# A Fourier mixing layer with a low-rank mixer: narrow products set side by side on TensorE, and another channel step for the second batch

## The chip, the cores and the metric

The kernel runs on one core of a Trainium2 chip. The core has five engines with a queue each: TensorE (PE; its weight loads are listed as PEld), VectorE (DVE), ScalarE (ACT), GpSimd (POOL) and SyncE (SP), which here only issues DMAs. The metric is the device time of one execution in microseconds (us).

## The reference

The input `x` is 8 x 3136 x 256 (batch, sequence, channel). The first stage takes the real part of a Fourier transform over sequence and channel; the second is a mixer:

```
X = real(fft(fft(x, axis=1), axis=2))          # per batch 3136 x 256
u = X + V^T (U^T X)                            # low rank, rank 32, over the sequence
out = u + relu(u @ w_ch1) @ w_ch2              # 256 -> 1024 -> 256 channels
```

## The kernel before

**Transform over the sequence.** The real part is cos·cos - sin·sin, and both factors are symmetric, so that 1569 of 3136 output rows and 129 of 256 channels carry everything. For each batch DVE folds `x` along the channels (`along_d`, L344; the middle channel, number 128, is a single column that POOL copies in `alone`, L352), along the sequence (`mirror`, L356), and over two halves (`half`, L360). The result is two tiles `G[b % 2][par]` of eight tiles of 98 or 99 rows each; columns 0 to 127 belong to the sine, 128 to 255 to the cosine, 256 is channel 128 alone. The stationary operand of a product is such a column block of G, the moving one is a row of a cosine or sine table with 393 frequencies and, after them, 32 columns of the transformed U (`tabs`, 425 columns in all, QW). `seq` (L399) does one of eight groups of a batch: par (even or odd frequencies), typ (0 sine, 1 cosine) and pn (odd or even rows). The pn=0 group is copied to `ev` by ACT, the pn=1 group is combined with it on DVE into the tiles `A` (cosine) and `B` (sine).

**Channel 128.** It needs the cosine alone. In batches 0 and 1 (b < B0 = 2) the sine groups get four more products each (L420), with columns 256 to 383 of G as the stationary operand and the cosine table as the moving one; since those columns are zero except the first, the result for channel 128 lands in row 0 of `B`. Batches 2 to 7 take channel 128 together in a *column pass* (`column_steps`, L485): its `x` values come by small DMAs, `fold_c` folds them to `GC[par]` with six columns for each of the eight tiles, and `group` (L507) runs four groups (par, pn) of four products with a stationary operand of six columns. The pn=0 groups are copied by ACT, the pn=1 groups are combined by DVE into `rows`, one row per batch; `finish` mirrors `rows` on ACT and puts the low-rank part into `tabc128`.

**Transform over the channels.** Batch 0 uses `chan` (L535): for four stretches of 392 rows and two halves h, one product of `A` with the cosine matrix `MC` and one of `B` with the sine matrix `MSN` are summed, and the sum is copied to `S` (h=0, by ACT) or `T` (h=1, by DVE). Batches 1 to 7 use `even_ch` (L547) and `odd_ch` (L556): `A` with `ME` is copied to `evd` by ACT, `B` with `MO` stays in PSUM, and DVE forms the sum as S and the difference as T. `across` (L565) then copies rows 64 to 127 of `A`, straight and mirrored, into rows 64 to 127 of `VA[b % 2]`, and for batch 1 also row 0 of `B` (channel 128) into row 32 of it; batches 2 to 7 get row 32 by a DMA from `rows` (L585). For batch 0 `last_row` (L588) writes row 64 of VA on DVE instead. `MO` is `MSN` with its row 0 set to zero by POOL.

**Mixer.** `lowrank` (L573) makes `TA` for a batch. The batches' rows are cut into 49 chunks of 512. `front(c)` (L606) multiplies `VA` with `TA` and DVE adds S or T: that is `u`. `first_product` (L626, eight per chunk, relu on ACT) and `second_product` (L636, four per chunk, on DVE the sum with `u`, which a DMA has transposed) are the mixer.

**Order.** Up to the first chunk the instructions run in the order written (`manual_schedule`, from L99 to `order.close()`, L860); after that a planner orders each engine's queue by its own model of times, starting from the order of the program, and the folds are pinned to the order written. The setup builds the tables (L694 to L813): POOL makes some of them by copies (`mirror_even`, `cosine_odd(4)`), issues the loads (`load_weights`, `load_v`, `load_second`), and runs `alone` for both halves of batch 0. From chunk 0 on each step of the next batch hangs on a slot 8c + j (chunk c, first product j): `spread` (L841) deals the steps of `fold`, `transform` and `column_steps` over a range of slots. Batch 1's transform has slots 23 to 42, the column pass 56 to 68. `front(c + 1)` is issued at j = 3.

**PSUM.** Every product outside the two mixer products takes one of three buffers with the tag "dft": `pt`, `pth`, `ptc`, `pst`, `ptt`, `ph`. A buffer is free again when ACT or DVE has read it for the last time.

In the setup there is already a function that runs narrow products in four groups of 32 output partitions, `transform_u` (L264):

```
for n in range(NI // 2):
    for g in range(4):
        pk, pn = divmod(g, 2)
        i = ktiles(pk)[n]
        nc.tensor.matmul(acc[g * R:(g + 1) * R, :], GU[:kp(i), typ, pn, i, :],
                         tabs[typ][:kp(i), i, pn, :NQ],
                         start=(n == 0), stop=(n == NI // 2 - 1))
```

Of the kernel before, what the change touches and what calls it, by code (L numbers as in the profile page):

```python
# [10 lines left out]
BF16 = mybir.dt.bfloat16  # L11
# [5 lines left out]
P = 128  # L17
PQ = 98
KP = PQ + 1
NI = 8  # L20
# [7 lines left out]
def kernel(  # L28
# [137 lines left out]
    def va_zeros(s):  # L166

        nc.gpsimd.memset(VA[s][R:2 * R].bitcast(I32), 0)
        if s == 0:
            nc.gpsimd.memset(VA[s][2 * R:].bitcast(I32), 0)  # L170

# [12 lines left out]
    ME = cpool.tile([P, P], BF16, name="me")  # L184
    MO = cpool.tile([P, P], BF16, name="mo")
    nc.vector.tensor_scalar(ncol[:], ncol[:], 1.0 / S, 0.0, op0=AL.mult, op1=AL.max)
# [71 lines left out]
    def ktiles(par):  # L258
        return [i for i in range(NI) if (i + 1) % 2 == par]
# [139 lines left out]
    def seq(b, par, typ, pn, parts=(0, 1)):  # L399
# [8 lines left out]
        g = G[b % 2][par]  # L408
        if pn == 0 and (b >= B0 or (b == 1 and typ == 1)):
            halves(d, g, par, typ)  # L410
            return
# [38 lines left out]
    cr = cpool.tile([KP, 2, NI, NB], FP32, name="cr")  # L450
    GC = [cpool.tile([KP, NI, NB], BF16, name=f"gc{par}", tag=f"gc{par}") for par in range(2)]
    rows = cpool.tile([NB, S], BF16, name="rows")
    tabc128 = cpool.tile([P, (NB + 3) * R], BF16, name="tabc128")
    flip = cpool.tile([P, 2, P], BF16, name="flip")
    unit = cpool.tile([P, NB], FP32, name="unit")

    def column_zeros():
        nc.gpsimd.memset(cf[:], 0.0)
        nc.gpsimd.memset(cr[:], 0.0)

    def column_flips():
# [3 lines left out]
    def column_loads():  # L465

        for t, dst, n in ((0, cf, NI - 1), (1, cr, 0)):
# [7 lines left out]
            for b in range(NB):  # L475
                for a in range(2):
# [6 lines left out]
                    yield load  # L483

    def column_steps():  # L485
        ec = cpool.tile([KP, 2, NI, NB], BF16, name="ec")
        tc_ = cpool.tile([NB, 2, R], FP32, name="tc")

        def fold_c():
# [11 lines left out]
            for par in range(2):  # L501
                nc.vector.tensor_tensor(GC[par][:], ec[:, 0], ec[:, 1],
                                        op=AL.add if par == 0 else AL.subtract)
        yield fold_c
        ev = {}

        def group(par, pn):  # L507
            pt = psum.tile([NB, QW], FP32, tag="dft", name="ptc", bufs=3)
            ks = ktiles(pn)
            for n, i in enumerate(ks):  # L510
                nc.tensor.matmul(pt[:], GC[par][:kp(i), i, :], tabs[1][:kp(i), i, par, :],  # L511
                                 start=(n == 0), stop=(n == len(ks) - 1))
            if pn == 0:
                ev[par] = wp.tile([P, QW], FP32, tag="ev", name="evc", bufs=2)
                nc.scalar.copy(ev[par][:NB], pt[:])
                return
            e = ev[par][:NB]
            up = rows[:, HALF // 2 - par:(0 if par else None):-2]
            dn = rows[:, HALF // 2 + 2 - par:HALF + 1 - par:2]
            nc.vector.tensor_tensor(up, pt[:, par:NQ], e[:, par:NQ], op=AL.add)  # L520
            nc.vector.tensor_tensor(dn, e[:, 1:NQ], pt[:, 1:NQ], op=AL.subtract)
            nc.vector.tensor_tensor(tc_[:, par, :], pt[:, NQ:QW], e[:, NQ:QW], op=AL.add)
        for par in range(2):
            for pn in range(2):
                yield lambda par=par, pn=pn: group(par, pn)

        def finish():
            nc.scalar.copy(rows[:, HALF + 1:S], rows[:, HALF - 1:0:-1])
            nc.vector.tensor_tensor(tc_[:, 0], tc_[:, 0], tc_[:, 1], op=AL.add)
            for b in range(NB):  # L530
                nc.vector.tensor_single_scalar(tabc128[:NB, b * R:(b + 1) * R], tc_[:, 0],
                                               unit[:NB, b:b + 1], op=AL.mult)
        yield finish

# [21 lines left out]
    def odd_ch(b, ch):  # L556
        d = ST[b]
        lo = ch * 392 + (1 if ch else 0)
        hi = (ch + 1) * 392 + 1
        pt = psum.tile([P, NQ], FP32, tag="dft", name="pst", bufs=3)  # L560
        nc.tensor.matmul(pt[:, :hi - lo], MO[:], d["B"][:, lo:hi], start=True, stop=True)  # L561
        for k, op in (("S", AL.add), ("T", AL.subtract)):
            nc.vector.tensor_tensor(d[k][:, lo:hi], d["e"][:, :hi - lo], pt[:, :hi - lo], op=op)  # L563

    def across(b, to, src, ch):  # L565

        lo = ch * 392 + (1 if ch else 0)
        hi = (ch + 1) * 392 + 1
        nc.scalar.copy(VA[b % 2][to, lo:hi], src[:, lo:hi])
        lo, hi = max(lo, 1), min(hi, HALF)  # L570
        nc.scalar.copy(VA[b % 2][to, S - hi + 1:S - lo + 1], src[:, hi - 1:lo - 1:-1])

    def lowrank(b):  # L573
        d = ST[b]
        pt = psum.tile([P, 256], FP32, tag="dft", name="ptt", bufs=3)
        n = 0
        for typ in range(2):
            for par in range(2):
                nc.tensor.matmul(pt[:], TAB[:, (2 * typ + par) * R:(2 * typ + par) * R + P],  # L579
                                 MDT[typ][:],  # L580
                                 start=(n == 0), stop=(n == 3 and b < B0))
                n += 1
        if b >= B0:
            nc.tensor.matmul(pt[:], tabc128[:, (b - B0) * R:(b - B0) * R + P], ones[:], start=False, stop=True)
            nc.sync.dma_start(out=VA[b % 2][R:R + 1, :], in_=rows[b - B0:b - B0 + 1, :])  # L585
        nc.scalar.copy(TA[b % 2][:R, :], pt[:R])
# [80 lines left out]
    def transform(b):  # L667

        for par, typ in ([(0, 0), (1, 0), (0, 1), (1, 1)] if b == 0 else
                         [(0, 1), (0, 0), (1, 1), (1, 0)]):  # L670
            for pn in range(2):
                yield lambda par=par, typ=typ, pn=pn: seq(b, par, typ, pn)
        if b == 0:
            for ch in range(4):
                for h in range(2):
                    yield lambda ch=ch, h=h: chan(b, ch, h)
            return
        for ch in range(4):
            yield lambda ch=ch: (even_ch(b, ch), across(b, slice(2 * R, P), ST[b]["A"][2 * R:], ch))
            yield lambda ch=ch: (odd_ch(b, ch),  # L680
                                 b < B0 and across(b, slice(R, R + 1), ST[b]["B"][0:1], ch))
        yield lambda: lowrank(b)
# [29 lines left out]
    cosine_low(1)  # L712
    mirror_even(0, 1)
    load_weights()
    cosine_odd(4)
    halve(0)
# [36 lines left out]

    alone(0, xr, EOR_)
    alone(0, xf, EOF_)
    load_v()
# [8 lines left out]
    ta_rows(0)  # L765
    alone(1, xr, EOR_)
    alone(1, xf, EOF_)
    uc[0]()
# [33 lines left out]
    column_zeros()  # L802
    nc.gpsimd.memset(tabc128[:].bitcast(I32), 0)

    def channel_tables():
# [3 lines left out]
        nc.gpsimd.memset(ME[QD:, 0:1], 0.0)  # L809
        nc.gpsimd.tensor_copy(MO[:], MSN[:, :P])  # L810
        nc.gpsimd.memset(MO[0:1], 0.0)

# [25 lines left out]

    due = {0: steps[6:7], 1: steps[7:8], 2: [lambda: last_row(0), column_flips]}

# [61 lines left out]
```

## Time and profile before

| | |
|---|---|
| median of three runs | 463.79 us (462.05 to 465.17) |
| the profiled execution | 463.73 us |
| its span, from first to last instruction | 462.0 us |
| busy: PE, DVE, ACT, POOL | 444.9, 353.1, 299.8, 69.7 us |
| mean granted clock of TensorE | 0.996 |

A row of the profile gives the start and length in us (or, for groups, the count, the busy time and the mean length in ns of one), the engine, the line of the kernel, the operation, what it writes and reads, and the shape. In brackets stands how long the engine sat idle before, and whose work ended that. A line with `x16` merges 16 instructions that follow one another. A length of a product is longer than its share of PE's time, because products overlap; starts are what to compare. DVE's and ACT's instructions overlap by about 0.1 us too.

### The profile page before, as it was taken

Reading aid. Unit: us, or ns where it says so; the run is one execution under the profiler, and the core shown is the slowest. Engines: PE = TensorE matmul, PEld = TensorE weight load, DVE = VectorE, ACT = ScalarE, POOL = GpSimd, SP = SyncE. Lnnn points to the kernel's source line nnn. Section 1 sums busy time; section 2 is a strip of 40 time slices with the busy share of each in tenths; the row PEclk is TensorE's granted clock in tenths of the full one; section 3 lists DMA queues with packets and bytes.
Section 4 is the critical chain, followed back from the end, with each engine's and each line's share of the span. In section 5 each row is a group of like instructions: output and inputs, shape, how many; then the busy total and the mean of one; then the engine's idle time right before and its main releaser. Section 6 shows DMA issues by size and latency. Waiting matters only on the chain.

```text
span 462.0 us, 8048 instructions
## 1 busy us (share of the span) xinstructions
PE 444.9 (96%) x2988; PEld 290.7 (63%) x2988; DVE 353.1 (76%) x811; ACT 299.8 (65%) x570; POOL 69.7 (15%) x112
## 2 busy tenths in 40 slices
PE   3889999899999999999999999999999999999996
PEld 2544656565666666666666666666666666666665
DVE  8887998886898779977898769977898666433433
ACT  7866537965876568655866577655865586656552
POOL 5992621020022001120022002100000000000000
PEclk9989999999999999999999999999999999999999
DMA  7994898994276824973377736683235323333343
GB/s 217 233 238 111 172 219 200 132 206 96 69 193 197 213 70 132 208 217 92 115 209 201 148 81 161 193 218 111 70 91 115 91 71 115 91 116 92 114 116 113
DMA packets 102955, 67.51 MB, mean 146 GB/s; under 512 B 73526, under 2 KB 99328, under 8 KB 99776
## 3 DMA queue, kind: packets, MB, share of 16 engines
q1 hardware_dynamic: 97906, 41.26, 38.3%
q0 software_dynamic: 4992, 25.74, 19.4%
q8 instruction: 23, 0.38, 0.3%
q14 instruction: 16, 0.13, 0.1%
q10 hardware_dynamic: 18, 0.00, 0.0%
HBM read 29.33 MB, written 25.69 MB: 119 GB/s over the span
## 4 chain that ended last, share of the span: by engine, by line
PE 87%; DVE 5%; POOL 2%; ACT 2%; issue 2%; DVEq 0%; POOLq 0%
PE p L648 35%; PE p L632 34%; PE pt L423 7%; PE ph L612 4%; PE pth L390 2%; DVE eor L348 1%; PE pst L561 1%; DVE eof L348 1%; PE pst L552 1%; DVE u L620 1%; PE ptt L579 1%; PE ptc L511 1%; DVE eos L357 1%; POOL xf L55 1%; ACT tabs L218 0%
## 5 line engine op out<-in xcount | busy, mean ns | idle before, releaser
L634 ACT ACTIVATE h<-p 128x512 bf16<-128x512 f32 x392 | 223.4, 597 | 130.3 <-PE p L632 128.4
L632 PE MATMUL p<-u,w 128*128 128x512 bf16 x784 | 218.8, 379 | 1.0 <-DVE u L620 0.8
L648 PE MATMUL p<-w,h 128*128 128x256 bf16 x1568 | 203.4, 273 | 0.0
L648 PEld LDWEIGHTS <-h 128*128 128x128 bf16 x1568 | 152.9, 98 | 59.9 <-issue 0.5
L632 PEld LDWEIGHTS <-w 128*128 128x128 bf16 x784 | 76.0, 98 | 52.4 <-issue 3.6
L654 DVE TENSOR_TENSOR o<-p,ut 128x4 f32<-128x4 f32 (+1 forms) x100 | 16.3, 163 | 58.8 <-PE p L648 56.3
L55 POOL DMA_INDIRECT xf<-in_x_dram,xidx x16 | 20.9, 1304 | 190.3 <-DVE eof L348 187.1
L657 DVE TENSOR_TENSOR o<-p,ut 128x254 f32<-128x254 f32 (+1 forms) x100 | 40.7, 407 | 0.0
L656 DVE TENSOR_TENSOR o<-p,ut 128x254 f32<-128x254 f32 (+1 forms) x100 | 40.7, 407 | 0.0
L348 DVE TENSOR_TENSOR eor<-xr 99x1024 bf16<-99x1024 f32 x32 | 39.1, 1230 | 0.0
L348 DVE TENSOR_TENSOR eof<-xf 99x1024 bf16<-99x1024 f32 x32 | 38.5, 1217 | 0.0
L620 DVE TENSOR_TENSOR u<-ph,S 128x512 bf16<-128x512 f32 (+15 forms) x64 | 35.1, 557 | 0.0
L620 DVE TENSOR_TENSOR u<-ph,T 128x512 bf16<-128x512 f32 (+15 forms) x64 | 35.0, 557 | 0.0
L423 PEld LDWEIGHTS <-g 98*128 98x128 bf16 (+1 forms) x184 | 18.3, 100 | 19.7 <-issue 2.3
L612 PE MATMUL ph<-va,ta 128*128 128x512 bf16 (+18 forms) x128 | 29.6, 329 | 0.6 <-ACT evd L554 0.6
L563 DVE TENSOR_TENSOR S<-evd,pst 128x392 bf16<-128x392 f32 (+1 forms) x28 | 15.8, 563 | 9.7 <-PE pst L561 7.8
L357 DVE TENSOR_TENSOR eos<-eof,eor 99x1024 bf16<-99x1024 bf16 (+2 forms) x33 | 21.9, 676 | 1.6 <-POOL eof L354 1.5
L423 PE MATMUL pt<-tabc,g 98*128 98x425 bf16 x104 | 22.2, 343 | 0.1
L423 PE MATMUL pt<-tabs,g 98*128 98x425 bf16 x80 | 19.1, 370 | 1.5 <-DVE g L361 1.5
L361 DVE TENSOR_TENSOR g<-eos 99x2048 bf16<-99x2048 bf16 (+3 forms) x20 | 19.8, 1008 | 0.2
L432 DVE TENSOR_TENSOR tab<-pt,ev 128x32 bf16<-128x32 f32 x32 | 6.1, 191 | 17.7 <-PE pt L423 16.7
L563 DVE TENSOR_TENSOR T<-evd,pst 128x392 bf16<-128x392 f32 (+1 forms) x28 | 15.7, 560 | 0.0
(157 smaller groups left out, 332.3 us busy)
## 6 DMA issues: line engine op xcount, KB each, us to landing
out_dram<-o SPq DMA_DIRECT2D x48, 512.0 KB
xr<-in_x_dram POOLq DMA_DIRECT2D x14, 784.0 KB, 6.3
xr<-in_x_dram SPq DMA_DIRECT2D x2, 784.0 KB
ut<-u SPq DMA_TRANSPOSE x49
w<-in_moe_w_ch_dram SPq DMA_DIRECT2D x1, 512.0 KB
w<-in_moe_w_ch_dram POOLq DMA_DIRECT2D x1, 512.0 KB, 5.7
out_dram<-o SPq DMA_DIRECT2D x4, 128.0 KB
va<-in_moe_V_dram POOLq DMA_DIRECT2D x2, 196.0 KB, 5.3
```

What stands on the lines that cost most here:

```text
L55: nc.gpsimd.indirect_dma_start(out_, None, bass.AP(t.tensor, t.offset, [[w, rows], [1, w]]), bass.IndirectOffsetOnAxis(idx, 0), element_of ...
L348: pin(nc.vector.tensor_tensor(dst[:, a, :, part * P:(part + 1) * P].rearrange("p i (k t) -> p i k t", k=2), lo, hi, op=AL.subtract if part ...
L357: pin(nc.vector.tensor_tensor(EOS[:, a, :, cols], EOF_[:, a, :, cols], EOR_[:, a, ::-1][:, :, cols], op=op))
L423: nc.tensor.matmul(pt[:], g[:kp(i), i, col:col + P], tabs[t][:kp(i), i, par, :], start=(n == 0), stop=(n == len(mm) - 1))
L563: nc.vector.tensor_tensor(d[k][:, lo:hi], d["e"][:, :hi - lo], pt[:, :hi - lo], op=op)
L612: nc.tensor.matmul(ph[:, col:col + hi - lo], TA[b % 2][:, s * P:(s + 1) * P], VA[b % 2][:, lo:hi], start=True, stop=True)
L620: nc.vector.tensor_tensor(u[:, s, col:col + hi - lo], ph[:, col:col + hi - lo], src, op=AL.add)
L632: nc.tensor.matmul(p1[:], W1[:, s, j * P:(j + 1) * P], k["u"][:, s, :], start=(s == 0), stop=(s == 1))
L634: LAST[0] = nc.scalar.activation(k["h"][:, j, :], p1[:], AF.Relu)
L648: nc.tensor.matmul(p2[:, t % w, :], h[:, j, rs], W2[:, j, :], start=(j == 0), stop=(j == JT - 1))
L656: nc.vector.tensor_tensor(o[:, ts, 1:P], p2[:, :w, 1:P], ut[:, ts, 1:P], op=AL.add)
L657: nc.vector.tensor_tensor(o[:, ts, P + 1:D], p2[:, :w, P + 1:D], ut[:, tT, P - 1:0:-1], op=AL.add)
```

## The change

- **Narrow products.** A new function `narrow` replaces `group`. It runs all 16 products of a single-channel transform in one step: the four groups (pn, par) write four bands of 32 partitions of one PSUM tile. The stationary operand is 32 columns wide, of which the first nb count. ACT copies the lower 64 partitions (pn = 0) to the upper half of `ev`; two further steps, one for each par, combine the halves on DVE, straight into `dst`. The column pass uses it with six columns; `GC` gets 32 zeroed columns behind it, so that its last block can be read 32 wide.
- **Batch 1's channel 128** leaves the sine groups (four products less in each of four) and uses `narrow` with columns 256 to 287 of G. Its row goes to row 32 of `VA[1]`, mirrored by two ACT copies, and its low-rank part to `low`, so that `lowrank(1)` has a fifth product.
- **Batch 1's channel step** is now `chan`, with both halves copied by ACT, and `last_row(1)`; rows 64 to 127 of `VA[1]` are zeroed by POOL in the setup.
- `MO` goes: `odd_ch` uses `MSN` directly.
- **Order.** In the setup POOL runs `alone` for half 0 before `cosine_odd(4)` and `load_weights`, and for half 1 before `load_v`. `column_flips` (two DVE copies) moves from slot 2 to slot 44. Batch 1's transform has 21 steps instead of 17, the column pass 5 instead of 6, in the same ranges of slots.

```
     def va_zeros(s):
         nc.gpsimd.memset(VA[s][R:2 * R].bitcast(I32), 0)
-        if s == 0:
-            nc.gpsimd.memset(VA[s][2 * R:].bitcast(I32), 0)
+        nc.gpsimd.memset(VA[s][2 * R:].bitcast(I32), 0)
...
-            if b < B0:
+            if b == 0:
                 mm += [(1, 256, i) for i in ktiles(1 - pn)]
...
+    def narrow(nb, stationary, dst, tc_):
+        t = {}
+        def products():
+            pt = t["pt"] = psum.tile([P, QW], FP32, tag="dft", name="ptc", bufs=3)
+            for n in range(NI // 2):
+                for g in range(4):
+                    pn, par = divmod(g, 2)
+                    i = ktiles(pn)[n]
+                    nc.tensor.matmul(pt[g * R:(g + 1) * R], stationary(par, i),
+                                     tabs[1][:kp(i), i, par, :],
+                                     start=(n == 0), stop=(n == NI // 2 - 1))
+            t["ev"] = wp.tile([P, QW], FP32, tag="ev", name="evc", bufs=2)
+            nc.scalar.copy(t["ev"][2 * R:], t["pt"][:2 * R])
+        yield products
+        def sums(par):
+            e, o = (t[k][(2 + par) * R:(2 + par) * R + nb] for k in ("ev", "pt"))
+            up = dst[:, HALF // 2 - par:(0 if par else None):-2]
+            dn = dst[:, HALF // 2 + 2 - par:HALF + 1 - par:2]
+            nc.vector.tensor_tensor(up, o[:, par:NQ], e[:, par:NQ], op=AL.add)
+            nc.vector.tensor_tensor(dn, e[:, 1:NQ], o[:, 1:NQ], op=AL.subtract)
+            nc.vector.tensor_tensor(tc_[:, par], o[:, NQ:QW], e[:, NQ:QW], op=AL.add)
+            if par:
+                nc.vector.tensor_tensor(tc_[:, 0], tc_[:, 0], tc_[:, 1], op=AL.add)
+        for par in range(2):
+            yield lambda par=par: sums(par)
...
+        yield from narrow(NB, lambda par, i: GC[par][:kp(i), i * NB:i * NB + R], rows, tc_)
...
+    def first_channel():
+        tc_ = cpool.tile([1, 2, R], FP32, name="tc1")
+        dst = VA[1][R:R + 1]
+        yield from narrow(1, lambda par, i: G[1][par][:kp(i), i, 256:256 + R], dst, tc_)
+        def finish():
+            mid = (HALF + S) // 2
+            for lo, hi in ((HALF + 1, mid), (mid, S)):
+                nc.scalar.copy(dst[:, lo:hi], dst[:, S - lo:S - hi:-1])
+            nc.vector.tensor_copy(low[:1, :R], tc_[:, 0])
         yield finish
...
-        nc.tensor.matmul(pt[:, :hi - lo], MO[:], d["B"][:, lo:hi], start=True, stop=True)
+        nc.tensor.matmul(pt[:, :hi - lo], MSN[:, :P], d["B"][:, lo:hi], start=True, stop=True)
...
+        if b > 0:
+            nc.tensor.matmul(pt[:], low[:, (b - 1) * R:(b - 1) * R + P], ones[:], start=False,
+                             stop=True)
...
-        if b == 0:
+        if b == 1:
+            yield from first_channel()
+        if b < B0:
             for ch in range(4):
                 for h in range(2):
                     yield lambda ch=ch, h=h: chan(b, ch, h)
+            if b == 1:
+                yield lambda: (lowrank(b), last_row(b))
             return
...
     mirror_even(0, 1)
+    alone(0, xr, EOR_)
+    alone(0, xf, EOF_)
+    cosine_odd(4)
     load_weights()
-    cosine_odd(4)
...
-    alone(0, xr, EOR_)
-    alone(0, xf, EOF_)
+    alone(1, xr, EOR_)
+    alone(1, xf, EOF_)
     load_v()
...
-    due = {0: steps[6:7], 1: steps[7:8], 2: [lambda: last_row(0), column_flips]}
+    due = {0: steps[6:7], 1: steps[7:8], 2: [lambda: last_row(0)], 44: [column_flips]}
```

More of the change, by code (lines that the diff above doesn't have):

```diff
@@ L450 @@
     cr = cpool.tile([KP, 2, NI, NB], FP32, name="cr")
-    GC = [cpool.tile([KP, NI, NB], BF16, name=f"gc{par}", tag=f"gc{par}") for par in range(2)]
+    GC = [cpool.tile([KP, NI * NB + R], BF16, name=f"gc{par}", tag=f"gc{par}") for par in range(2)]
     rows = cpool.tile([NB, S], BF16, name="rows")
-    tabc128 = cpool.tile([P, (NB + 3) * R], BF16, name="tabc128")
+    low = cpool.tile([P, (NB + 4) * R], BF16, name="low")
     flip = cpool.tile([P, 2, P], BF16, name="flip")
@@ L459, in column_zeros @@
         nc.gpsimd.memset(cr[:], 0.0)
+        for par in range(2):
+            nc.gpsimd.memset(GC[par][:, NI * NB:], 0.0)
     def column_flips():
@@ L483, in column_loads @@
                     yield load
+    def narrow(nb, stationary, dst, tc_):
[21 more added lines that the diff above has]
+                nc.vector.tensor_tensor(tc_[:, 0], tc_[:, 0], tc_[:, 1], op=AL.add)
+        for par in range(2):
+            yield lambda par=par: sums(par)
     def column_steps():
@@ L501, in fold_c @@
             for par in range(2):
-                nc.vector.tensor_tensor(GC[par][:], ec[:, 0], ec[:, 1],
+                nc.vector.tensor_tensor(GC[par][:, :NI * NB].rearrange("p (i b) -> p i b", b=NB), ec[:, 0], ec[:, 1],
                                         op=AL.add if par == 0 else AL.subtract)
         yield fold_c
[L505 to L522, printed above, removed]
@@ L523, in column_steps @@
[L523 to L525 removed]
+        yield from narrow(NB, lambda par, i: GC[par][:kp(i), i * NB:i * NB + R], rows, tc_)
         def finish():
             nc.scalar.copy(rows[:, HALF + 1:S], rows[:, HALF - 1:0:-1])
[L529 removed]
             for b in range(NB):
[L531 removed]
+                nc.vector.tensor_single_scalar(low[:NB, (b + 1) * R:(b + 2) * R], tc_[:, 0],
@@ L765 @@
     ta_rows(0)
-    alone(1, xr, EOR_)
-    alone(1, xf, EOF_)
     uc[0]()
@@ L802 @@
     column_zeros()
-    nc.gpsimd.memset(tabc128[:].bitcast(I32), 0)
+    nc.gpsimd.memset(low[:].bitcast(I32), 0)
     def channel_tables():
```

21 lines of the change are left out of this document (9 added, 12 removed).

## The prediction

> **What bounds the kernel now.** I read the chain that ended last by engine, then busy time in stretches, then the order in time where an engine waits.
>
> ```profile
> PE 87%; DVE 5%; POOL 2%; ACT 2%; issue 2%; DVEq 0%; POOLq 0%
> ```
>
> TensorE (PE) carries the chain almost everywhere. Where it does not is seen in the stretches (columns: stretch, length, busy us of PE, PEld, DVE, ACT, POOL, granted clock, DMA share, GB/s):
>
> ```profile
> 26.00:28.00 2.00, 2.00 (x8) 0.77 (x7) 2.00 (x4) 0.09 (x1) 1.96 (x2) 0.50 0.91 274
> ...
> 62.00:75.00 13.00, 12.90 (x83) 7.85 (x82) 12.86 (x27) 5.32 (x12) 1.57 (x2) 1.00 0.92 197
> 75.00:91.00 16.00, 14.21 (x95) 9.13 (x94) 12.18 (x27) 15.65 (x33) 1.08 (x2) 1.00 0.88 149
> ...
> 104.00:119.00 15.00, 14.96 (x97) 8.37 (x96) 10.00 (x30) 7.89 (x18) 0.00 (x0) 1.00 0.45 108
> ...
> 120.00:170.00 50.00, 50.00 (x347) 33.62 (x346) 41.93 (x93) 33.74 (x67) 6.03 (x8) 1.00 0.60 158
> ```
>
> In the last two rows PE does not pause: from the column pass on, a microsecond of PE work less there is a microsecond less at the end. From 75 to 91 us, batch 1's channel step, ACT is full (15.65 of 16) and PE idles 1.8 us. From 62 to 75 us PE and DVE are both full. In the setup PE runs at half clock for a while. The change touches all four places.
>
> **The change part by part.** *Setup: the single-column copies ahead of the weight loads.* In order of time (start, length, engine, line; in brackets idle time and its releaser):
>
> ```profile
> 15.32 1.59 POOL L309 COPY tabs<-tabs 99x392 bf16<-99x392 bf16 x1
> ...
> 19.86 0.26 POOL L354 CAST eof<-xf 99x8 bf16<-99x8 f32 x1
> ...
> 32.81 0.87 POOL L807 TENSOR_SCALAR mc<-mc 1x256 bf16<-1x256 bf16 x1
> ```
> ```profile
> 17.71 1.21 DVE L348 TENSOR_TENSOR eof<-xf 99x1024 bf16<-99x1024 f32 x1
> 20.15 0.70 DVE L357 TENSOR_TENSOR eos<-eof,eor 99x1040 bf16<-99x1040 bf16 x1 [1.23 <-POOL eof L354]
> ```
> ```profile
> 22.44 0.92 PE L287 MATMUL put<-sel,wu 128*98 128x64 bf16 x8
> 24.83 4.02 PE L423 MATMUL pt<-tabs,g 98*128 98x425 bf16 x12 [1.47 <-DVE g L361]
> 28.68 2.33 PE L423 MATMUL pt<-tabc,g 98*128 98x425 bf16 x12
> ...
> 36.18 0.38 PE L579 MATMUL ptt<-mc,tab 128*128 128x256 bf16 x2
> ```
>
> POOL reaches the two copies at 19.7 us, behind two weight loads and a table copy; DVE waits 1.23 us for the second, and PE, behind DVE, starts batch 0's transform at 24.83. With the copies first, POOL does them at about 17.0 to 17.4. Their inputs are there: DVE reads `xf` half 0 without waiting before 17.71. So the fold runs 1.23 us earlier and PE starts at 23.6, just behind its last work (22.44 + 0.92 = 23.36). The second pair of copies moves ahead of V's load and finishes about 20.4; that half was loaded by a gather issued at 3.85 that takes 11 us:
>
> ```profile
> 3.85 0.99 POOL L55 DMA_INDIRECT xf<-in_x_dram,xidx  x1 [0.30 <-issue]
> DMA to landing us min/median/max: 11.0/11.1/11.2
> ```
>
> What the copies move past: the weights' two loads (later by the copies and the table copy, about 1.3 us; issued near 18 and not converted on ACT before 28), V's two loads, G's memset and batch 1's first loads (later by the second pair, 0.4 us, and not read by DVE before 42): covered by those gaps, and worth at most 1.3 if they were not. If a copy had to wait for its input, the table copy and all those loads would queue behind it on POOL; the landings above leave over 1 us. The rows also show 12 products in 4.02 us at clock 0.50, then 12 in 2.33. After 1.47 us of idle the clock fell and came back at 28.7. With a gap of 0.2 us I expect no fall, which is worth up to another 4.02 - 2.17 = 1.8 us (0.181 us each when warm). But the low-rank product needs POOL's halved MC, done at 33.68; POOL's queue is full from 15 us on, gains two small memsets (GC's padding) and hardly moves. Against 36.18 that caps the gain at 2.5 us. Bounds: 1.2 (DVE's wait alone) and 2.5; I take **-2.1**, nearer the cap, as evictions follow one another on DVE and ACT.
>
> By the Trainium skill ("TensorE: Matmul & The Clock Gate", "Why this matters for your kernels") PE goes back to half clock after idle gaps above about 3 us. By that rule a gap of 1.47 us would not have cooled it, and shortening it would not keep it warm; the first rival takes this up.
>
> *Column flips and POOL's memsets.*
>
> ```profile
> 43.15 0.29 DVE L462 CAST flip<-fl 128x256 bf16<-128x256 f32 x1
> 27.30 1.41 POOL L170 MEMSET va<- 64x1568 int32 x1
> 60.32 0.39 PE L632 MATMUL p<-u,w 128*128 128x512 bf16 x1 [0.53 <-DVE u L620]
> ```
>
> DVE has no pause from 43 to 61 us and PE waits for it at 60.32, so the 0.3 us that the flips leave is taken once: **-0.3** (0 to -0.5). They come back at step 44, about 93 us, in DVE's slack. VA[1]'s second memset (1.41 us) delays POOL's copies for batch 1 by less than 1.4 us from 37.2; the sum that reads them runs at 50.5: nothing. Without that cover it would be 1.4.
>
> *Batch 1.* PE loses 16 products of 425 columns (four groups, pn by par), and 8 channel products become 16:
>
> ```profile
> 73.69 0.89 PE L423 MATMUL pt<-tabs,g 98*128 98x425 bf16 x4
> 74.42 0.89 PE L423 MATMUL pt<-tabc,g 98*128 98x425 bf16 x4
> ...
> 81.61 0.38 PE L612 MATMUL ph<-va,ta 128*128 128x512 bf16 x1 [0.65 <-ACT evd L554]
> 85.75 0.33 PE L561 MATMUL pst<-B,mo 128*128 128x392 bf16 x1 [1.15 <-ACT evd L554]
> 85.92 0.33 PE L552 MATMUL pst<-A,me 128*128 128x392 bf16 x1
> ```
> ```profile
> 20.99 0.85 PE L274 MATMUL pu<-tabc,gu 98*32 98x393 bf16 x16 [0.32 <-ACT tabc L311]
> 21.78 0.67 PE L732 MATMUL idle<-tabs 98*128 98x393 bf16 x3
> ```
>
> The first start-to-start is 0.73 for four, 0.181 each: 16 less are -2.90. The four-abreast form is in this trace already: 16 narrow products from 20.99 until the next work at 21.78, 0.79 us; for 425 columns 0.85, and with 0.09 for entering the form (see the columns below) +0.93. Eight channel products more at 0.17 (85.75 to 85.92): +1.33. One product of 256 columns for the low-rank sum: +0.11. Together **-0.53**.
>
> The two waits (0.65 and 1.15) stand where ACT is full. ACT loses and gains:
>
> ```profile
> L554 ACT COPY evd<-pst 128x392 f32<-128x392 f32 x3 | 1.4, 482 | 0.0
> L569 ACT COPY va<-A 64x392 bf16<-64x392 bf16 x3 | 1.6, 519 | 0.0
> L569 ACT COPY va<-B 1x392 bf16<-1x392 bf16 x3 | 1.6, 520 | 0.0
> ...
> 118.59 1.50 ACT L528 COPY rows<-rows 6x1567 bf16<-6x1567 bf16 x1 [0.26 <-DVE rows L521]
> ```
>
> Four evictions and 16 copies across go (4 x 0.48 + 16 x 0.52 = 10.2 us of lengths); eight channel copies of the evictions' shape (8 x 0.48), one eviction (0.5) and a mirrored row in two pieces (1.5 to 1.6) come: 6.0. ACT is 4 us lighter and stops being full. DVE loses 8 sums and gains the row's sums and the last row:
>
> ```profile
> L563 DVE TENSOR_TENSOR S<-evd,pst 128x392 bf16<-128x392 f32 x3 | 1.7, 567 | 1.8 <-PE pst L561 1.7 <-ACT evd L554 0.2
> L590 DVE TENSOR_TENSOR va<-S,T 1x1567 bf16<-1x1567 bf16 x1 | 1.0, 967 | 0.1
> L520 DVE TENSOR_TENSOR rows<-ptc,evc 6x393 bf16<-6x393 f32 (+1 forms) x2 | 1.2, 580 | 0.2 <-PE ptc L511 0.2
> L522 DVE TENSOR_TENSOR tc<-ptc,evc 6x32 f32<-6x32 f32 x2 | 0.3, 166 | 0.0
> ```
>
> 8 x 0.57 = 4.5 go; 4 x 0.58 + 4 x 0.17 + 0.97 + a short copy = 4.1 come (six partitions cost what 128 do, 580 against 567 ns, so one partition should too). DVE is not relieved, and in 62 to 75 us it is as full as PE, so part of PE's saving meets DVE. Of the 1.8 us of waits I take **-1.2**; bounds 0.5 worse (the new copies wait in ACT's queue behind the relus) and -1.8.
>
> *Column pass.*
>
> ```profile
> 105.53 0.88 PE L423 MATMUL pt<-tabc,g 98*128 98x425 bf16 x4
> 106.35 0.89 PE L511 MATMUL ptc<-tabc,gc 98*6 98x425 bf16 x4
> 107.16 0.60 PE L632 MATMUL p<-u,w 128*128 128x512 bf16 x2
> ...
> 116.28 0.89 PE L511 MATMUL ptc<-tabc,gc 98*6 98x425 bf16 x4
> 117.09 0.60 PE L632 MATMUL p<-u,w 128*128 128x512 bf16 x2
> ```
>
> Four wide products from 105.53 end at 106.26; the next narrow group starts 0.09 later and lasts 0.81 until 107.16. So each group costs 0.90 and four of them 3.6. One group of 16 abreast costs 0.93: -2.7. PE is full here, so it counts whole, less the price of a PSUM buffer: the product now stays in one of three buffers ("dft") from its step until the second half of its sums, five steps later, where a group was emptied within two. The bound is one wait like the longest above, 1.15; I take 0.2. **-2.5** (-2.7 to -1.5).
>
> **Sum**: -2.1 - 0.3 - 0.5 - 1.2 - 2.5 = -6.6, from the profiled execution's 463.73 (span 462.0 and 1.7 around it; the median of the runs is 463.79): **457.1 us**, -1.4%. About 1% is what a measurement of this kernel tells from no change.
>
> **The rivals.**
> 1. *The clock falls all the same*: the setup gives only the 1.23 us, sum 458.0. For it: the fall's cause is inferred from one row of one execution. Against: the earlier gaps of 0.3 to 0.6 us cooled nothing. Chance 0.13.
> 2. *DVE becomes the bound in batch 1*: from 62 to 75 us it is at 12.86 of 13, its work does not shrink, and the first u of batch 1 waits behind the folds of batch 2 and now also the last row (0.97). Then the waits are not won and the 0.5 of PE is lost too, plus one more wait in the columns (1.15): 457.1 + 1.2 + 0.5 + 0.95 = 459.8, up to 462 if the setup gives only its lower bound and the last row adds its length. For it: DVE's share; against: 3.4 us of idle in DVE's 75 to 91. Chance 0.22.
> 3. *Slower: the held PSUM buffer.* While a narrow product waits for two rounds of sums, wide products, u's inputs and channel products share two buffers, each freed by DVE or ACT. Every allocation that then waits costs up to the 1.15 us of 85.75. Six waits eat the gain; ten to twelve, from both holds and the bunching behind them, give +5 to +7, 462 to 471, about 469 at ten and a half. Against: a hold spans about five allocations in the column pass and none or two in batch 1, and DVE frees within 1 to 2 us. Chance 0.10. The Trainium skill says ("TensorEngine Tiling (Array Packing)", "PSUM Bottleneck") that packing speeds up TensorE but not the emptying of PSUM, which may become the bottleneck; no row of before shows this.
> 4. *The products do not run abreast*: 16 x 0.181 = 2.9 instead of 0.93 twice, +3.9: 461.0. The row at 20.99 speaks against it. Chance 0.03.
>
> The forecast itself, 455.3 to 459, has 0.52.
>
> **How the numbers follow.** Faster by over 1% means below 459.15: the forecast, rival 1 and a fifth of rival 2, less the tail of the first two, 0.63. Within 1%: most of rival 2, rival 4 and that tail, 0.28. Slower by over 1% (above 468.4): rival 3, most of it, 0.09. The range leaves out rival 3 and the far tails: 454.8 (all terms at their good ends, -2.5 - 0.5 - 0.5 - 1.8 - 2.7 = -8.0, give 455.7, and a little for the run's own spread) to 461.5.
>
> **What would show it.** DVE's 1.23 us wait gone and PE's first wide product near 23.6; granted clock 1.00 from 24 to 29; low-rank product near 33.7; two groups of 16 narrow products of about 0.85 us; ACT below 14 of 16 us in batch 1's channel step, and PE without the waits of 0.65 and 1.15; the column stretch 2.5 us shorter. It is wrong if PE waits for a "dft" buffer around the narrow products, if u of batch 1 comes late on DVE, or if POOL's copies wait for data at 17 us and hold DVE as before.

## The result, and the profile after

The changed kernel takes 459.59 us (median of four runs, 458.64 to 460.85) against 463.8 before; the ratio is 0.991, with a 95% interval of 0.9886 to 0.9941. The profiled execution has 459.99 us and a span of 458.2. The prediction was 457.1 in a range of 454.8 to 461.5: the time lies in the range, the gain is two thirds of the forecast, and at 0.9% it stays below the 1% that the prediction took as the least to be told from no change, where the forecast leaned to "faster". In runs 8 and 9 below, two of ten executions each were over 1.5% above the fastest and are left out of the medians.

Five products mark the same points of both programs: the low-rank product of batch 0, the front of the chunk that first wraps in batch 0 (33 columns), the front that begins batch 1 (64 columns), the second half of the column fold (99x48), and the front of the next wrap (97 columns). Their starts before, in order of time (the first is the row at 36.18 in the prediction):

```profile
55.70 0.62 PE L612 MATMUL ph<-va,ta 128*128 128x33 bf16 x4
91.34 0.60 PE L612 MATMUL ph<-va,ta 128*128 128x64 bf16 x4
104.30 0.23 PE L498 MATMUL pc<-cb,flip 99*99 99x48 bf16 x2
120.87 0.61 PE L612 MATMUL ph<-va,ta 128*128 128x97 bf16 x4
```

and after:

```profile
36.39 0.38 PE L600 MATMUL ptt<-mc,tab 128*128 128x256 bf16 x2
55.92 0.62 PE L635 MATMUL ph<-va,ta 128*128 128x33 bf16 x4
89.35 0.60 PE L635 MATMUL ph<-va,ta 128*128 128x64 bf16 x4
102.27 0.20 PE L524 MATMUL pc<-cb,flip 99*99 99x96 bf16 x1 [0.17 <-ACT cb L521]
103.26 0.23 PE L527 MATMUL pc<-cb,flip 99*99 99x48 bf16 x2 [0.67 <-ACT cb L522]
117.14 0.60 PE L635 MATMUL ph<-va,ta 128*128 128x97 bf16 x4
```

Differences of neighbouring marks give the account, in us:

| stretch | before | after | difference | predicted |
|---|---|---|---|---|
| start to the low-rank product | 36.18 | 36.39 | +0.2 | -2.1 |
| to the front of 33 columns | 19.52 | 19.53 | 0.0 | -0.3 |
| to the front of batch 1 | 35.64 | 33.43 | -2.2 | -1.7 |
| to the column fold | 12.96 | 13.91 | +0.95 | 0 |
| to the front of 97 columns | 16.57 | 13.88 | -2.7 | -2.5 |
| to the end of the span | 341.1 | 341.1 | 0.0 | 0 |

The sum is -3.75, which is the difference of the spans (-3.8). So both parts that concern products work, the setup gives nothing, and in front of the column fold a new wait takes back a part. In the busy times by stretch (columns as in the prediction) the rows that answer to those of before are below; the one from 91 to 104 us was, before,

```profile
91.00:104.00 13.00, 13.00 (x91) 8.60 (x90) 11.46 (x25) 7.87 (x17) 3.37 (x4) 1.00 0.96 209
```

and after:

```profile
62.00:75.00 13.00, 12.85 (x92) 8.11 (x94) 12.26 (x29) 5.74 (x12) 1.56 (x2) 1.00 0.80 165
75.00:91.00 16.00, 15.78 (x115) 9.69 (x106) 15.34 (x32) 12.69 (x26) 3.23 (x4) 1.00 0.82 152
91.00:104.00 13.00, 12.05 (x86) 8.22 (x86) 9.01 (x22) 7.70 (x17) 1.08 (x2) 1.00 0.96 202
104.00:119.00 15.00, 14.79 (x113) 9.49 (x113) 13.78 (x45) 10.35 (x20) 0.00 (x0) 1.00 0.44 131
```

ACT, full before from 75 to 91 us (15.65 of 16), is at 12.69; PE has gone from 14.21 to 15.78. From 91 to 104 us, where PE was full before, it now pauses for 0.95.

The setup shows why it gave nothing. In order of time, POOL, DVE and PE of the changed kernel:

```profile
16.86 0.67 POOL L352 CAST eor<-xr 99x8 bf16<-99x8 f32 x1
17.45 0.41 POOL L352 CAST eof<-xf 99x8 bf16<-99x8 f32 x1
17.78 1.84 POOL L321 COPY tabc<-tabs 99x784 bf16<-99x784 bf16 x1
...
23.71 1.00 POOL L164 MEMSET g<- 99x504 int32 x2
...
34.38 0.87 POOL L833 TENSOR_SCALAR mc<-mc 1x256 bf16<-1x256 bf16 x1
```
```profile
19.02 1.15 DVE L355 TENSOR_TENSOR eos<-eof,eor 99x1040 bf16<-99x1040 bf16 x1
...
24.29 1.29 DVE L359 TENSOR_TENSOR g<-eos 99x1024 bf16<-99x1024 bf16 x2 [1.01 <-POOL g L164]
...
49.72 0.29 DVE L462 CAST flip<-fl 128x256 bf16<-128x256 f32 x1
```
```profile
25.04 4.02 PE L421 MATMUL pt<-tabs,g 98*128 98x425 bf16 x12 [1.69 <-DVE g L359]
```

Before, POOL cleared the rest of G at 21.04:

```profile
21.04 1.03 POOL L164 MEMSET g<- 99x504 int32 x2
```

DVE no longer waits for the single-column copies (19.02, no bracket). But POOL now clears the rest of G at 23.71, and DVE's first write into G waits 1.01 us for that memset. One wait has gone and another has come, and PE starts at 25.04 instead of 24.83.

The two narrow steps (the line gives start and length of 16 products), the first in batch 1 and the second in the column pass, with PE's next work behind each:

```profile
74.67 0.91 PE L495 MATMUL ptc<-tabc,g 98*32 98x425 bf16 x16
75.74 0.81 PE L655 MATMUL p<-u,w 128*128 128x512 bf16 x3 [0.16 <-DVE B L438]
...
105.30 0.91 PE L495 MATMUL ptc<-tabc,gc 98*32 98x425 bf16 x16
106.37 0.38 PE L655 MATMUL p<-u,w 128*128 128x512 bf16 x1 [0.16 <-issue]
```

Each takes 1.07 us from its first start to the next work, of which 0.16 is a pause; the prediction had 0.85 to 0.93.

### The profile page after: what moved, and what is told of

It is laid out like the page before. It is cut to its first block, busy times and chain, and to the rows that moved or that the text cites. A ratio compares the mean times of both kernels' runs of the same rounds, so it can differ in the third digit from the quotient of the medians.

```text
span 458.2 us, 8001 instructions
## 1 busy us (share of the span) xinstructions
PE 438.9 (96%) x2944; PEld 289.7 (63%) x2997; DVE 353.6 (77%) x812; ACT 295.3 (64%) x560; POOL 68.6 (15%) x113
## 4 chain that ended last, share of the span: by engine, by line
PE 81%; DVE 8%; POOL 3%; issue 3%; DMA 2%; ACT 2%; SPq 1%; DVEq 0%; POOLq 0%; ACTq 0%
PE p L671 34%; PE p L655 31%; PE pt L421 6%; PE ph L635 4%; PE pth L388 2%; DVE eor L346 1%; DVE u L643 1%; DVE eof L346 1%; DMA ut<-u 1%; PE pst L572 1%; SPq L479 1%; PE pst L581 1%; PE ptt L600 1%; DVE eos L355 1%; DVE o L680 1%
## 5 line engine op out<-in xcount | busy, mean ns | idle before, releaser
L655 PE MATMUL p<-u,w 128*128 128x512 bf16 x733 | 209.6, 379 | 2.3 <-DVE u L643 1.0
L635 PE MATMUL ph<-va,ta 128*128 128x512 bf16 (+14 forms) x126 | 29.2, 328 | 0.2
L421 PEld LDWEIGHTS <-g 98*128 98x128 bf16 (+1 forms) x168 | 16.8, 100 | 18.3 <-issue 2.1
L421 PE MATMUL pt<-tabc,g 98*128 98x425 bf16 x88 | 18.7, 343 | 0.1
L583 DVE TENSOR_TENSOR S<-evd,pst 128x392 bf16<-128x392 f32 (+1 forms) x24 | 13.6, 567 | 6.5 <-PE pst L581 6.1
L73 POOL DMA_DIRECT2D xr<-in_x_dram x14 | 8.1, 576 | 38.6 <-DVE eor L346 38.5
```

What stands on the lines that cost most here:

```text
L421: nc.tensor.matmul(pt[:], g[:kp(i), i, col:col + P], tabs[t][:kp(i), i, par, :], start=(n == 0), stop=(n == len(mm) - 1))
L635: nc.tensor.matmul(ph[:, col:col + hi - lo], TA[b % 2][:, s * P:(s + 1) * P], VA[b % 2][:, lo:hi], start=True, stop=True)
L655: nc.tensor.matmul(p1[:], W1[:, s, j * P:(j + 1) * P], k["u"][:, s, :], start=(s == 0), stop=(s == 1))
```

## The experiments

All kernels are the changed one with one edit, if nothing else is said.

**The clock explains most of the spread.** A run's mean granted clock comes in steps of about 0.004, and its time follows. Runs of the kernel before: 462.1 us at 1.000, about 463.75 at 0.996, 465.3 to 465.6 at 0.993 in most. The changed kernel: 458.64 at 1.000, 459.19 and 459.99 at 0.996, 460.85 at 0.992. So small differences are best read at one clock, or between the marks of two profiles. At 1.000 the change is worth 3.5 us (one run of it), at 0.996 about 4.2.

**1. POOL's old order.** The copies go back behind the weight loads, each half's just ahead of where they stood before; all else stays.

```
-    alone(0, xr, EOR_)
-    alone(0, xf, EOF_)
-    cosine_odd(4)
     load_weights()
+    cosine_odd(4)
...
-    alone(1, xr, EOR_)
-    alone(1, xf, EOF_)
+    alone(0, xr, EOR_)
+    alone(0, xf, EOF_)
...
+    alone(1, xr, EOR_)
+    alone(1, xf, EOF_)
```

> The changed kernel with POOL's setup order of before (weight loads first, single-column copies later, flips and all else as changed). If the moved copies only traded DVE's wait for the copies (1.23 us) against a wait for G's memset (1.01 us), DVE waits 1.2 us for the copy again, the first wide product starts at 24.8 us instead of 25.04, and the time is within 0.5 us of 459.6. If the reordering did bring the 2.1 us of the prediction in some hidden way, the time is near 461.7.

Measured: 460.43 us (nine runs; 458.97 to 459.9 for four at clock 0.995 or 0.996, one of 461.61, and 460.4 to 460.8 at 0.991 or 0.992, against 459.2 to 460.0 and 460.85 of the changed kernel). The first product starts at 24.89 and the low-rank product at 36.24, 0.15 earlier than in the changed kernel. The median is 0.8 above the changed kernel's because four of the nine runs have the lower clock. DVE waits for the copy again and not for the memset:

```profile
20.15 0.70 DVE L355 TENSOR_TENSOR eos<-eof,eor 99x1040 bf16<-99x1040 bf16 x1 [1.23 <-POOL eof L352]
```
```profile
24.89 3.54 PE L421 MATMUL pt<-tabs,g 98*128 98x425 bf16 x12 [1.53 <-DVE g L359]
```

The reordering was worth nothing: it traded one wait for the other.

**2. G's memset early.** It moves into POOL's idle stretch at the start.

```
     nc.gpsimd.memset(pint[0:1], P)
+    g_zeros(0)
...
     load_v()
-    g_zeros(0)
```

> The changed kernel with G's memset for batch 0 moved into POOL's idle stretch at 8 to 11.7 us. If that memset, queued behind the moved copies and loads, is what took the place of the removed wait, DVE's first g starts near 23.3 instead of 24.29 and the first wide product near 24.0 instead of 25.04; the time falls by 1.0 us, to 458.6, and by up to 1.8 more if the shorter gap keeps the clock up. If POOL and DVE slow each other down or another input is late, the first product stays at 24.8 or later and the time at 459.6.

Measured: 458.28 us; 457.4 at clock 1.000, 1.2 below the changed kernel's run at that clock, about the 1.0 of the first reading. Another cause could give most of it: with the memset gone from ahead of it, POOL's halved MC is done at 33.3 instead of 35.25, and at full clock the low-rank product waits for MC (run 3 below). The profiled execution is a different one (clock 0.992, 460.56 us) and does not show the first reading:

```profile
7.75 1.61 POOL L164 MEMSET g<- 99x504 int32 x2
```
```profile
17.57 1.34 DVE L356 TENSOR_TENSOR eos<-eof,eor 99x1024 bf16<-99x1024 bf16 x1
24.25 1.29 DVE L360 TENSOR_TENSOR g<-eos 99x1024 bf16<-99x1024 bf16 x2
```
```profile
24.99 4.44 PE L422 MATMUL pt<-tabs,g 98*128 98x425 bf16 x12 [2.44 <-DVE g L360]
```

The wait for the memset is gone, yet DVE reaches G at 24.25. It is late earlier: the memset took 1.61 instead of 1.00, the fold of half 0 began 0.5 us later, and one of DVE's sums took 1.34, against 0.88 at this place in the changed kernel. Both expectations hold in part; how much of the setup's length is POOL and DVE slowing each other is not settled by this run.

**3. The gap filled.** Eight idle products ahead of batch 0's transform.

```
     uc[2]()
+    busy(8)
```

> The changed kernel with eight idle products (0.164 us each, 1.3 us) in PE's gap before batch 0's transform; they leave the computation alone. If the gap of 1.7 us is what lets the clock fall, the granted clock stays 1.00 from 25 to 29 us, the 12 wide products take 2.2 instead of 4.02 us, and the low-rank product starts 1.0 to 1.6 us earlier (POOL's halved MC at 35.25 caps it): about 458.4. If the clock falls for another reason, the 12 products still take 4.0 us and the time stays at 459.6.

Measured: 457.98 us, four runs within 0.4. The first wide products start as late as in the changed kernel, but at full clock (the second fence is the stretch from 26 to 28 us):

```profile
25.07 2.34 PE L421 MATMUL pt<-tabs,g 98*128 98x425 bf16 x12 [0.39 <-DVE g L359]
...
35.34 0.38 PE L600 MATMUL ptt<-mc,tab 128*128 128x256 bf16 x2 [0.41 <-POOL mc L834]
```
```profile
26.00:28.00 2.00, 2.00 (x13) 1.08 (x12) 2.00 (x3) 0.10 (x1) 1.80 (x7) 1.00 1.06 204
```

Twelve products in 2.34 us instead of 4.02, and the low-rank product held by POOL's halved MC, as the prediction's cap had it. The gap of 1.7 us is what costs the clock. The run-to-run spread goes with it.

Two of the later runs (5 and 6) have the changed kernel's setup without idle products. In their profiles PE's earlier work ended 0.4 to 0.6 us later, the gap was shorter, and the clock stayed at 1.00 from 24 to 30 us as well (run 5, then run 6):

```profile
25.12 2.34 PE L421 MATMUL pt<-tabs,g 98*128 98x425 bf16 x12 [1.13 <-DVE g L359]
```
```profile
25.13 2.34 PE L421 MATMUL pt<-tabs,g 98*128 98x425 bf16 x12 [1.39 <-DVE g L359]
```

There too the low-rank product waits 0.43 us for MC (35.41 and 35.42). In all the other profiles without idle products the gap ahead of the transform was 1.43 us or more, and the clock fell.

**4. The narrow products in another order.** All four products of a band in a row, instead of the bands in turn.

```
-            for n in range(NI // 2):
-                for g in range(4):
+            for g in range(4):
+                for n in range(NI // 2):
```

> The changed kernel with the same 16 narrow products in another order: group after group, so that neighbours share a band of 32 output partitions. If the gain comes from four bands running at once, each of the two steps takes 2.9 us instead of 0.85 and the time rises by 4 us, to 463.6. If products of 32 columns were quick for another reason (fewer instructions, fewer switches), it stays at 459.6.

Measured: 459.82 us, and at equal clock the same as the changed kernel. The 16 products take 0.94 us instead of 0.91:

```profile
74.35 0.94 PE L495 MATMUL ptc<-tabc,g 98*32 98x425 bf16 x16
75.44 0.81 PE L655 MATMUL p<-u,w 128*128 128x512 bf16 x3 [0.16 <-DVE B L438]
```

The rise of 4 us did not come, but that does not speak against four bands at once: the next run has products in one band alone. And the records of single products show four at a time in this order too. They start in rounds of four about 0.18 us apart; within a round they start 0.013 us apart here and 0.003 in the changed kernel, as if each band worked through its own four while the queue ran ahead.

**5. The column pass in four groups.** `narrow` stays for batch 1; the columns get `group` of before, six columns wide and always in the first band.

```
-        yield from narrow(NB, lambda par, i: GC[par][:kp(i), i * NB:i * NB + R], rows, tc_)
+        for par in range(2):
+            for pn in range(2):
+                yield lambda par=par, pn=pn: group(par, pn)
```

> The changed kernel with the column pass as before (four groups of four products, six columns wide, all in the first band of partitions); batch 1 stays changed. If four bands at once are what the columns gain, the stretch from the column pass' first product to the front of chunk 8 is 2.7 us longer and the time rises by 2.5 to 2.9 us, to 462.3. If the gain in that stretch came from fewer waits for the mixer's buffers and not from the bands, less than 1 us.

Measured: 462.3 us, +2.7 (462.2 and 462.6 in the two runs at clock 1.000, but 460.78 in the profiled one at 0.999, 2.1 above the changed kernel at 1.000). From the column fold to the front of 97 columns the profile has 101.36 to 117.93, 16.57 us, exactly as before, against 13.88. First and last group:

```profile
103.41 0.89 PE L540 MATMUL ptc<-tabc,gc 98*6 98x425 bf16 x4
...
113.33 0.89 PE L540 MATMUL ptc<-tabc,gc 98*6 98x425 bf16 x4
```

Four products in one band take 0.89 us, sixteen over four bands 0.91. So the bands do run at once, and it does not matter in which order they are issued.

**6. Batch 1's channel step as before.** Channel 128 stays narrow.

```
-        if b < B0:
+        if b == 0:
             for ch in range(4):
                 for h in range(2):
                     yield lambda ch=ch, h=h: chan(b, ch, h)
```

> The changed kernel with batch 1's channel step as before (even and odd products, sums on DVE, rows 64 to 127 copied across by ACT); channel 128 of batch 1 stays narrow. If ACT's load is what made PE wait in that step, ACT is at 14 of 16 us or more again and PE waits 0.5 to 1.8 us, against 1.33 us of PE work less: the time is within 1 us of 459.6. If PE's work alone decides, the time falls by 1.3 us, to 458.3.

Measured: 459.34 us, within the spread of the changed kernel. But the stretch to the front of batch 1 runs from 54.82 to 87.69, 32.87 us: 0.56 shorter than with `chan` (33.43, and 33.43 to 33.46 in every other profile with this `chan`). And ACT is not full:

```profile
75.00:91.00 16.00, 15.80 (x104) 9.79 (x103) 15.88 (x34) 12.09 (x25) 2.67 (x4) 1.00 0.83 134
```

No product of the channel step waits for an eviction, so the even and odd step need not fill ACT. Two things differ from before: the eight copies of a single row (0.52 us each) that carried channel 128 across are gone, and the eight copies of 64 rows run earlier, from 71.2 to 75.3 instead of 74.8 to 87.8 (ACT has 8.14 us from 62 to 75, against 5.32 before). Which of the two ended the waits, this run does not separate. The narrow channel is worth 2.8 us of this stretch (35.64 to 32.87), and `chan` costs 0.56 of it. The 0.56 does not last: from the front of 33 columns to the fold's second half, less the wait of 1.12 in front of it, this run takes 46.8 us and the changed kernel, less its 0.67, 46.7; the total shows no difference.

**7. The second half of the channel products on DVE.**

```
-        (nc.vector.tensor_copy if b == 0 and h == 1 else nc.scalar.copy)(
+        (nc.vector.tensor_copy if h == 1 else nc.scalar.copy)(
```

> The changed kernel with the second half of batch 1's channel products (T) copied by DVE, as for batch 0, instead of ACT. DVE stands at 27.6 of 29 us from 62 to 91 us and would get 4 copies of 0.57, 2.3 us, more than its 1.4 us of idle. If DVE is by now the bound of that stage, the front of batch 1 comes 0.9 us later or more and the time is 460.5. If PE is the bound and DVE's work can slide, it stays at 459.6.

Measured: 459.51 us, no change; the stretch to the front of batch 1 is 33.56 (55.99 to 89.55).

```profile
75.00:91.00 16.00, 15.97 (x115) 9.54 (x108) 15.71 (x32) 11.26 (x21) 2.66 (x4) 1.00 0.87 132
```

PE is at 15.97 of 16: PE's work is the bound there now, and DVE's folds slide. The second rival of the prediction is out.

**8 and 9. The column loads earlier.** First one per slot from slot 8 (the first added line), then at the old density from slot 4 (the second).

```
-        due.setdefault(8 + 5 * n // 4, []).append(step)
+        due.setdefault(8 + n, []).append(step)
+        due.setdefault(4 + 5 * n // 4, []).append(step)
```

> The changed kernel with the column pass' 28 small loads dealt one per slot from slot 8 instead of four per five slots, so that the last is issued eight slots earlier. If PE's waits of 0.17 and 0.67 us ahead of the column fold come from these loads landing late on SP's queue, they vanish and the time falls by 0.8 us, to 458.8. If ACT's own queue holds the two copies, they stay and so does the time.

> The changed kernel with the column loads at their old density (four per five slots) but from slot 4 instead of 8. If the loads simply land too late for a PE that is 2 us faster, the waits of 0.17 and 0.67 us ahead of the column fold vanish and no transpose of u is held up: 458.8. If these loads, wherever they are put, hold up the transposes on the same queue, DVE waits for a transposed u as in the dense version and the time is 460 or more.

Measured: medians of 462.2 and 462.4 us over eight executions each, with wide spreads (459.56 to 465.54; 458.01 to 464.76). A part of that is the clock, which was lower in more of these runs (the half rate lies at 24 to 32 us, ahead of these loads); at 1.000 the shifted one has 458.0 to 459.1, around the changed kernel's 458.64. The wait ahead of the fold is down to 0.17 in both, but the shifted one's profile has another:

```profile
101.87 0.17 DVE L677 TENSOR_TENSOR o<-p,ut 128x4 f32<-128x4 f32 x1 [4.70 <-DMA ut<-u]
```
```profile
90.56 3.56 SPq L646 DMA_TRANSPOSE ut<-u  x1
94.17 2.92 SPq L479 DMA_DIRECT2D cr<-in_x_dram  x2
97.19 0.65 SPq L685 DMA_DIRECT2D out_dram<-o  x1
97.95 3.61 SPq L646 DMA_TRANSPOSE ut<-u  x1
```

The loads and the transposes of u share SP's queue. Two transposes among the loads take 3.6 us each to issue instead of 1.3 (the one at 101.03 us of the changed kernel). That length alone is not the cause: in runs 3 and 10 one takes 4.1 and 4.3 us and nothing waits for it. Here the second is also issued late, at 97.95, behind the loads; DVE waits 4.7 us for a transposed u, the next u is late, and the stretch from batch 1's front to the fold is 15.63 us, longer than the 13.91 that was to be shortened.

**10 to 12. Put together.** Idle products and POOL's old order; the same with the dense loads; the same with the shifted ones.

> The changed kernel with POOL's setup order of before and the eight idle products, the column loads untouched. If POOL's moved copies only pushed the halved MC back (35.25 against 33.9), the low-rank product runs 0.8 us earlier than with the idle products alone (34.5 instead of 35.34) and the time is 457.2. If the faster setup only makes PE wait longer for the column loads ahead of the fold, it stays at 458.0.

> The changed kernel with POOL's setup order of before, eight idle products in PE's gap, and the column loads one per slot. If POOL's moved copies only pushed the halved MC back (35.25 against 33.9) and the gap alone costs the clock, the low-rank product starts at 34.5 to 34.7 without waiting for POOL, 0.8 us ahead of the run with idle products alone, and the column fold does not wait: 458.0 - 0.7 - 0.8 = 456.5. If the idle products and the order compete for the same gain, 458.0 stays.

> All three together: POOL's order of before, eight idle products, column loads from slot 4 at the old density. If the three waits are independent: 457.2 less up to 0.8, so 456.4 to 457.2. If the loads hold up transposes: 458 or more.

Measured: 457.52 us (five runs, 457.35 to 457.55, all at clock 1.000; ratio to before 0.986, 0.9845 to 0.9882), 459.43 (457.42 to 461.74) and 458.61 (457.58 to 459.14). The dense version is outside both of its expectations. Without the moved loads:

```profile
24.86 2.34 PE L421 MATMUL pt<-tabs,g 98*128 98x425 bf16 x12 [0.17 <-DVE g L359]
...
34.56 0.38 PE L600 MATMUL ptt<-mc,tab 128*128 128x256 bf16 x2
...
100.61 0.23 PE L527 MATMUL pc<-cb,flip 99*99 99x48 bf16 x2
```

The low-rank product no longer waits for MC and runs 0.8 us ahead of the run with idle products alone; of that 0.5 is left in the median. The fold's second half does not wait here. With the loads moved, DVE waits 4.9 (dense) and 3.9 us (shifted) for a transposed u, and the medians lose 1 to 2 us. The best version is the changed kernel without its reordering of POOL and with the gap filled.

## Why the prediction was right or wrong

**Setup, -2.1: wrong, it measured +0.2.** The step that failed is "what the copies move past ... G's memset ...: covered". The memset was pushed from 21.04 to 23.71, 2.7 us where the prediction allowed 0.4, and DVE's write into G waits for it (1.01 us), though the two touch different columns. That the copies' inputs had landed and that DVE's wait of 1.23 would go was right. What mis-sized the push is a second error: the copies' lengths were taken from rows in which DVE stood idle, waiting for them. Beside a working DVE the first pair and the table copy took 0.67, 0.41 and 1.84 instead of 0.26, 0.26 and 0.89, which is 1.7 us of the push, and the second pair took the other 1.0. With the lengths of before the memset would have ended near 22.5, ahead of DVE, which was ready at 23.28. In run 2's profile the wait for the memset is gone, DVE's own instructions are stretched instead, and nothing is gained there either. And with the gap not closed (1.69 us), the clock fell as before. The mechanism of the clock and the cap by MC were right, as the run with idle products shows; only this change does not get there. "POOL's queue ... hardly moves" was wrong as well: MC is done at 35.25 instead of 33.68, and at full clock that costs 0.8 us (34.56 against 35.34, runs 10 and 3).

**The clock.** Gaps of 1.47 us (before) and 1.69 us (after) cost half the clock for 3.4 us (worked out from 0.80, 0.50 and 0.85 in the three stretches of 2 us from 24 to 30), and filling the second kept it at 1.00. Over all the profiles, gaps up to 1.39 us kept it and gaps from 1.43 us lost it. The length of the gap is not all: in runs 8 and 9, with gaps of 1.76 and 1.72, the half rate lasted twice as long (0.50 from 26 to 30 us); what else decides is open. The Trainium skill ("TensorE: Matmul & The Clock Gate", "Why this matters for your kernels") allows idle gaps of about 3 us; the measurement differs from it and decides. The first rival (the clock falls all the same) came true in its result, but because the gap stayed, not because the gap did not matter.

**Flips, -0.3: nothing.** The planner placed the two copies at 49.72, inside the same full stretch of DVE. A slot is the earliest place in the program's order for a step, not a time, and these had no inputs to wait for.

**Batch 1, -1.7: -2.2, right in sign, with the cause in the wrong place.** Both waits (0.65 and 1.15) went, 1.8 rather than the 1.2 I allowed. But the relief of ACT was credited to the whole channel step; run 6 shows that the narrow channel alone ends the waits, with the even and odd step left as it was, and that the sixteen products cost 0.56 in this stretch.

**Column pass, -2.5: -2.7.** The arithmetic of the groups held; the held PSUM buffer cost nothing that the marks show. The third rival did not happen.

**Not foreseen: +0.95 ahead of the fold.** The column loads land when SP's queue lets them, in the changed kernel at 102.2. The last three loads on that queue, before, in the changed kernel and in run 3:

```profile
89.77 2.59 SPq L479 DMA_DIRECT2D cr<-in_x_dram  x3
```
```profile
95.17 5.75 SPq L479 DMA_DIRECT2D cr<-in_x_dram  x3
```
```profile
89.43 4.70 SPq L479 DMA_DIRECT2D cr<-in_x_dram  x3
```

The last is issued by 92.4 before and by 100.9 in the changed kernel: single issues took up to 3.75 us there, most others 0.8. So it is the late queue, and not only the earlier PE: in run 3 PE reaches the fold 2 us earlier still (101.1), the last load is issued by 94.1, and PE does not wait for it. What stretches the issues in some executions is open. The prediction left these loads out. The wait differs from execution to execution: 0.67 here, 1.13 and 1.12 in runs 4 and 6, none in the other profiles.

**The time in the range.** That the time lies in the range says little for the sum: the setup, a third of it, gave nothing, a wait that was not in it took 0.95, and the range was wide enough for both.

**The fourth rival** (not abreast) is out by run 5.

## What to carry to other kernels

When an instruction is moved ahead on a busy in-order queue, list everything that it passes with the time at which each is needed, also memsets of parts of a tile that another engine writes, and take lengths from rows in which the neighbouring engine works. Where the engine that bounds the kernel stands idle for a microsecond or two ahead of a dense stretch, filling the gap with idle products may be worth more than shortening it; here it gave 1.6 us in the median and a steady time. A saving of PE work can be lost again at the next transfer, so compare when the queue issues the transfers behind the stage that gets shorter, before and after, and over several executions.

## What the runs showed of the hardware that I had not expected

- POOL and DVE slow each other: a POOL copy of 99x784 took 0.89 us with DVE waiting and 1.84 beside it; DVE's 99x1040 sum took 0.70 and 1.15. Which of the two is stretched differs: in run 2 the same POOL copy took 0.83 beside a DVE sum that took 1.34 instead of 0.88.
- Sixteen products of 32 columns over four bands took 0.91 us with the bands in turn and 0.94 with each band's four in a row, while four in one band alone took 0.89.
- The times of equal programs come in steps that follow the granted clock: about 1.65 us for each half-rate stretch of about 3.4 us (462.1, 463.75 and 465.3 us before the change, at 1.000, 0.996 and 0.993).
- Among small loads on SP's queue, a transpose took 3.6 us to issue instead of 1.3 (run 9), and a small load up to 3.75 instead of 0.8 (the changed kernel).
